# A fused attention and feed-forward kernel: the first twelve chunks' k and q loaded as groups of 512 tokens

## The chip, the cores and the metric

The kernel runs on one core of a Trainium2 chip. Its time is the device time of one execution in microseconds (us); the number compared is the median of several runs. The core has five engines, each of which works through its own list of instructions in order: TensorE (PE, matrix products; PEld is its weight load), VectorE (DVE), ScalarE (ACT), GpSimd (POOL) and SyncE (SP). They wait for each other through semaphores. DMA transfers are issued from SP, ACT or POOL and are carried by 16 DMA engines. Matrix products are written to PSUM, a small memory next to TensorE; everything else lies in SBUF.

## The reference

The reference is sliding-window causal attention over 8 batches, 8 heads, 576 tokens and a head size of 64, followed by a feed-forward layer with a squared relu:

```python
scores = scale * np.matmul(q, k.transpose(0, 1, 3, 2))
rel = pos[:, None] - pos[None, :]
mask = (rel >= 0) & (rel < 64)
scores = np.where(mask, scores, -1e9)
attn = np.exp(scores - np.max(scores, axis=-1, keepdims=True))
attn = attn / (np.sum(attn, axis=-1, keepdims=True) + 1e-09)
attn_out = np.matmul(attn, v)
x = attn_out.transpose(0, 2, 1, 3).reshape(4608, 512)
h = np.maximum(x @ w_in, 0.0)        # w_in: 512 x 2048
out = h * h @ w_out                  # w_out: 2048 x 512
```

All inputs and the output are float32. q, k and v lie in memory as [batch, head, token, 64], so one token of one head is a run of 256 bytes, and consecutive tokens of one head follow each other.

## The kernel before, in words

The 4,608 tokens are worked in 36 *chunks* of 128 tokens; four chunks are a *group* of 512 tokens (9 groups). A chunk goes through these functions, whose short names are used in the order of the work:

- `load` (L77) issues the transfer of one chunk of k, q or v (256 KB: 128 partitions, one token each, with 8 runs of 256 bytes) into a staging tile `st` from a pool of 15. A chunk that crosses a batch boundary takes two transfers of 64 partitions.
- `cast_kq` (L94) and `cast_v` (L101) turn them into float16. `cast_v` has three POOL instructions per chunk: the values, and two copies moved by 64 partitions for the neighbouring window block.
- `transposes` (T, L158) brings k and q of a chunk to head-size-on-partitions with eight TensorE transposes; DVE copies kT and ACT copies qT out of PSUM, 512 elements per partition each. Every fourth chunk fills a boundary tile `kB`, which joins the last 64 keys of the group before with the first 64 of this one.
- `scores` (S, L183) makes 16 small products, two exponentials on ACT and two maskings (a minimum) on DVE.
- `values` (V, L208) multiplies by v with a column of ones for the denominator; DVE takes the reciprocal and multiplies.
- `to_xT` (X, L229) transposes the result back with TensorE, and DVE copies it out. From group 3 on this is a DMA transpose (`to_xT_xbar`), and from group 4 on k and q are transposed by DMA too (`transposes_xbar`).
- The up projection is `up_chunk` (U, L262: one chunk and one quarter of the 2,048 columns, 16 matmuls of 128 columns) for the first eight chunks, and `up` (L253: a whole group and 128 columns, 4 matmuls of 512 columns) later. Both end in `square`: relu on ACT, then a multiply on DVE. `up_chunk` writes to the pool `ps_up` of two PSUM banks, and for odd quarters of the chunks below 6 to `ps_out`'s two banks as well.
- `out_proj` (L281) takes one chunk and one quarter of `w_out`: 4 matmuls of 512 columns. After the fourth quarter ACT copies the sum out and SP issues the store.

Nothing reorders the work: on every engine the instructions stand in the order in which the program calls these functions. The first part is written out by hand. It issues the loads of chunks 0 to 3 in the order k, q, v per chunk (the first q from ACT's queue), then goes through chunks 0 to 5 with `warm` matmuls (products of zeros that keep TensorE busy) in the gaps. The four quarters of w_in and of w_out are loaded from POOL's queue (`load_w_in` L116, `load_w_out` L121; read as float32, written as float16, 1 MB read each), between the POOL casts; the first three quarters of w_in stand behind the casts of v of chunks 0 to 2 and of k of chunk 3. Then `run` (L365) sorts a list of (place, function, arguments) by place, a number between 0 and 1, and calls them: one such list for the out projection of group 0 with the attention of chunks 6 to 11 and the up projection of chunks 6 and 7 (L372 to L380), and one list per later group (L381 to L404), in which `out_proj` of one group alternates with `up` of the next and the attention of the one after.

A staging tile, an `st`, can be loaded again when its cast has read it, and the queue of SP stands still while the instruction at its head waits.

Of the kernel before, what the change touches and what calls it, by code (L numbers as in the profile page):

```python
# [16 lines left out]
def kernel(  # L17
# [37 lines left out]

    NV = 8
    FQ = DFF // 4
    KQ_XBAR = 4
    X_XBAR = 3

# [16 lines left out]
    def load(src, i, eng=None):  # L77

        st = stage.tile([P, H, D], FP32, name="st", tag="st")
        for (p0, p1, b, t0) in pieces(i):  # L80
            (eng or nc.sync).dma_start(  # L81
                out=st[p0:p1], in_=src[b, :, t0:t0 + p1 - p0, :].rearrange("h p d -> p h d"))
        return st

    kqs, kTs, kBs, qTs = {}, {}, {}, {}

    def group_tile(d, pool, key, g, shape, nm):
        if (key, g) not in d:
            d[key, g] = pool.tile(shape, FP16, name=nm, tag=nm)
        return d[key, g]  # L90
# [5 lines left out]
    def cast_kq(key, i, st, copy):  # L96

        copy(out=kq16(key, i // 4)[:, :, i % 4, :].rearrange("p a (b d) -> p a b d", d=D),  # L98
             in_=st[:].rearrange("p (a b) d -> p a b d", b=2))

    def cast_v(i, st):  # L101

        v_ev, v_od, v_next = v_evs[i % NV], v_ods[i % NV], v_ods[(i + 1) % NV]
        nc.gpsimd.tensor_copy(out=v_ev[:, :, 0:D], in_=st[:])  # L104
        nc.gpsimd.tensor_copy(out=v_od[64:P, :, 0:D], in_=v_ev[0:64, :, 0:D])  # L105
        if i + 1 < NCK:
            nc.gpsimd.tensor_copy(out=v_next[0:64, :, 0:D], in_=v_ev[64:P, :, 0:D])  # L107
# [31 lines left out]
        return group_tile(xTs, xtp, "x", g, [P, 2, DMC, 256], "xT")  # L139

    def kT_of(g):
        new = ("k", g) not in kTs
        t = group_tile(kTs, ktp, "k", g, [P, HP, 512], "kT")
        if new:
            kB = group_tile(kBs, ktp, "b", g, [P, HP, P], "kB")
            if g >= KQ_XBAR:
                pass
            elif g > 0:
                nc.vector.tensor_copy(out=kB[:, :, 0:64], in_=kTs["k", g - 1][:, :, 448:512])
            else:  # L150
                nc.vector.memset(kB[:, :, 0:64], 0.0)
        return t

    def qT_of(g):

        return group_tile(qTs, ktp, "q", g, [P, HP, 512], "qT")

    def transposes(i):  # L158
        g, a = i // 4, i % 4 * P
        ps = ps_att.tile([P, 2, 4, P], FP16, name="qkT_ps", tag="ps_a")  # L160
        for s, key in enumerate("kq"):
            for c in range(4):
                nc.tensor.transpose(out=ps[:, s, c, :], in_=kqs[key, g][:, c, i % 4, :],
                                    identity=ident[:])
# [3 lines left out]
        nc.scalar.activation(out=q_dst, in_=q_src, func=AF.Copy, scale=1.0)  # L168
        if i % 4 == 0:
            nc.vector.tensor_copy(out=kBs["b", g][:, :, 64:P], in_=kTs["k", g][:, :, 0:64])  # L170

    def transposes_xbar(g):
        for key, dst in (("k", kT_of(g)), ("q", qT_of(g))):
# [2 lines left out]
                in_=kqs[key, g][:].rearrange("p a c t -> p (a c t)"))  # L176

    def boundary(g):
        kB = kBs["b", g]
        nc.vector.tensor_copy(out=kB[:, :, 0:64], in_=kTs["k", g - 1][:, :, 448:512])  # L180
        nc.vector.tensor_copy(out=kB[:, :, 64:P], in_=kTs["k", g][:, :, 0:64])

    def scores(i):  # L183
# [77 lines left out]

    def up_chunk(i, fq):  # L262
        g, t0, a = i // 4, i % 4 * P, i % 2 * P
        pool, tag = (ps_out, "ps_o") if fq % 2 and i < 6 else (ps_up, "ps_u")
        hps = pool.tile([P, 4, P], FP32, name="hps4", tag=tag)
        for f in range(4):
            for c in range(DMC):
                nc.tensor.matmul(  # L268
                    hps[:, f, :], w_in_q[fq][:, c, f * P:(f + 1) * P],
                    xT_of(g)[:, i % 4 // 2, c, a:a + P], start=(c == 0), stop=(c == DMC - 1))  # L270
# [31 lines left out]
    for i in range(1, 4):  # L302
        sts[i] = [load(x, i) for x in (k, q, v)]
    make_identity(nc, ident[:])
    nc.gpsimd.memset(base[:], BIG)
    nc.gpsimd.affine_select(
# [14 lines left out]
    warm(8)  # L321
    cast_kq("k", 0, sts[0][0], nc.vector.tensor_copy)
    cast_kq("q", 0, sts[0][1], nc.scalar.copy)
    cast_v(0, sts[0][2])

    def cast_chunk(i):
        cast_kq("k", i, sts[i][0], nc.gpsimd.tensor_copy)
        cast_kq("q", i, sts[i][1], nc.scalar.copy)
        cast_v(i, sts[i][2])

    T, S, V, X, U = transposes, scores, values, to_xT, up_chunk
    T(0), warm(3)
    cast_chunk(1)
    S(0), warm(3), T(1), warm(1)
    cast_chunk(2)
    V(0), S(1), warm(2), X(0), T(2), warm(1)
    cast_kq("k", 3, sts[3][0], nc.gpsimd.tensor_copy)
    for quar in range(3):
        load_w_in(quar)
    cast_kq("q", 3, sts[3][1], nc.scalar.copy)  # L340
    cast_v(3, sts[3][2])
    sts[4] = [load(x, 4) for x in (k, q, v)]
    cast_kq("k", 4, sts[4][0], nc.gpsimd.tensor_copy)
    load_w_in(3)
    cast_kq("q", 4, sts[4][1], nc.gpsimd.tensor_copy)
    cast_v(4, sts[4][2])
    sts[5] = [load(x, 5) for x in (k, q, v)]
    cast_kq("k", 5, sts[5][0], nc.gpsimd.tensor_copy)
    load_w_out(0)
    load_w_out(1)  # L350
    cast_kq("q", 5, sts[5][1], nc.gpsimd.tensor_copy)
    cast_v(5, sts[5][2])
    load_w_out(2)
    load_w_out(3)
    V(1), S(2), X(1), warm(1), T(3), V(2), S(3), U(0, 0), X(2), U(1, 0), U(2, 0), V(3)
    load_chunk(6)
    U(0, 1), U(1, 1), X(3), U(2, 1), U(0, 2), U(1, 2), U(2, 2), U(3, 0), U(3, 1), T(4)
    load_chunk(7)
    U(3, 2), U(0, 3), S(4), U(1, 3), U(2, 3), U(3, 3), V(4), T(5), X(4), S(5)
    load_chunk(8)  # L360
    U(4, 0), U(4, 1), U(4, 2), V(5), U(4, 3), X(5), U(5, 0), U(5, 1), U(5, 2), U(5, 3)
    load_chunk(9)
    load_chunk(10)

    def run(steps):  # L365

# [3 lines left out]
            fn(*args)  # L370

    pairs = [(ts, fq) for a in (0, 2) for fq in range(4) for ts in (a, a + 1)]  # L372
    steps = [((n + 0.5) / 16, out_proj, 0, ts, fq) for n, (ts, fq) in enumerate(pairs)]
    for i in range(6, 12):
        t = 0.17 + 0.115 * (i - 6)
        steps += [(t, T, i), (t + 0.06, S, i), (t + 0.15, V, i), (t + 0.21, X, i)]
    steps += [(0.42 + 0.05 * fq, U, 6, fq) for fq in range(4)]
    steps += [(0.65 + 0.05 * fq, U, 7, fq) for fq in range(4)]
    steps += [(0.1 + 0.13 * n, load_chunk, i) for n, i in enumerate(range(11, 16))]
    run(steps)  # L380
    for g in range(2, NTB + 1):  # L381
        G = g + 1
        steps = [((n + 0.5) / 16, out_proj, g - 1, n // 4, n % 4) for n in range(16)]
        if g < NTB:
            steps += [((f + 0.8) / 16, up, g, f) for f in range(FFC)]
        if G < NTB:
            if G >= KQ_XBAR:
                steps += [(0.02, boundary, G), (0.05, S, 4 * G)]
            for j in range(4):
                i, t = 4 * G + j, 0.18 * j  # L390
                if G < KQ_XBAR:
                    steps += [(t, T, i), (t + 0.07, S, i)]
                steps.append((t + 0.17, V, i))
# [12 lines left out]

# [28 lines left out]
```

## Time and profile before

| | |
|---|---|
| median of 3 runs | 335.68 us (334.15 to 335.7) |
| the profiled execution | 335.83 us, of which the span from first to last instruction is 333.8 |
| PE busy | 307.7 us (92%) |
| DVE, ACT, POOL busy | 186.0, 156.3, 116.9 us |
| SP's DMA queue (q1) | 150,128 packets, 45.89 MB |
| POOL's DMA queue (q0: w_in, w_out) | 4,224 packets, 4.19 MB written |
| loads of k, q, v | 256 KB each, 4.7 to 5.2 us from issue to landing (median) |
| w_in, w_out quarters | 10.2 and 10.7 us from issue to landing (median) |

The profile page gives the busy share of each engine in 40 equal slices of the span, in tenths; the row PEclk is the clock that TensorE was granted, and the row DMA the mean busy share of the 16 DMA engines. The chain is the work that ended last, followed back from the end, at each step to what released it; its columns are start, length and what. In a timeline row the columns are start, length, engine, line, operation, out<-in, sizes and count; brackets hold the idle time before it and what ended that. In the table of windows each engine has its busy time and its number of instructions.

### The profile page before, as it was taken

To read this page: it belongs to the slowest core of one execution; us is meant where nothing else is said; L and a number is where in the kernel's file an instruction comes from. 1 tells how busy PE (TensorE), PEld (TensorE's weight loads), DVE (VectorE), ACT (ScalarE), POOL (GpSimd) and SP (SyncE) were. 2 spreads that over 40 slices of the span, in tenths; PEclk is the share of its full clock that TensorE was granted. 3 is DMA by queue.
4 is the path that set the end of the run, shared out by engine and by line. 5 is a ranking of instruction groups with operands and counts; after the bars stand their busy time and mean duration, and the time that the engine had idled before them with its cause. 6 is when DMAs were issued, how large, how long until landed. Compare 5 with 4: busy or idle time off the path is not lost.

```text
span 333.8 us, 7260 instructions
## 1 busy us (share of the span) xinstructions
PE 307.7 (92%) x2883; PEld 166.2 (50%) x2883; DVE 186.0 (56%) x431; ACT 156.3 (47%) x274; POOL 116.9 (35%) x191
## 2 busy tenths in 40 slices
PE   6749968999899999999999999999999999999995
PEld 2438857566644544444454444444444444444442
DVE  4645676478766664674476466647574665444300
ACT  3533553454645454454454455445544564344411
POOL 3761914876607160626063315423460000000000
PEclk9787998999999999999999999999999999999999
DMA  9999999999449769968979796989599121200111
GB/s 170 218 182 209 184 189 219 212 197 222 93 117 168 164 120 234 180 148 185 229 136 222 150 229 125 222 162 230 120 187 213 40 63 22 74 31 33 54 73 63
DMA packets 155425, 50.80 MB, mean 152 GB/s; under 512 B 146688, under 2 KB 150784, under 8 KB 155392
## 3 DMA queue, kind: packets, MB, share of 16 engines
q1 hardware_dynamic: 150128, 45.89, 67.7%
q0 software_dynamic: 4224, 4.19, 7.8%
q8 instruction: 22, 0.36, 0.5%
q10 hardware_dynamic: 1040, 0.26, 0.4%
q14 instruction: 11, 0.09, 0.1%
HBM read 36.70 MB, written 9.44 MB: 138 GB/s over the span
## 4 chain that ended last, share of the span: by engine, by line
PE 58%; DMA 14%; DVE 11%; SPq 7%; ACT 4%; POOL 2%; issue 2%; ACTq 0%; POOLq 0%
PE ops L285 26%; PE hps L256 20%; DMA qT<-q 7%; PE hps L268 7%; DMA st<-in_v_dram 5%; SPq L81 4%; DVE h L250 4%; ACT hrelu L249 3%; PE sc L193 3%; PE av L217 3%; DVE pm L206 2%; DVE x_sb L222 2%; SPq L174 2%; DMA w_in<-in_moe_w_in_dram 2%; POOL v_ev L104 1%
## 5 line engine op out<-in xcount | busy, mean ns | idle before, releaser
L250 DVE SCALAR_TENSOR_TENSOR h<-hps,hrelu 128x512 f16<-128x512 f32 x144 | 99.1, 690 | 109.7 <-ACT hrelu L249 109.3
L285 PE MATMUL ops<-w_out,h 128*128 128x512 f16 x576 | 145.5, 379 | 0.6 <-DVE h L250 0.6
L249 ACT ACTIVATE hrelu<-hps 128x512 f32<-128x512 f32 x144 | 86.0, 598 | 101.0 <-PE hps L256 81.6
L256 PE MATMUL hps<-xT,w_in 128*128 128x512 f16 x448 | 115.1, 379 | 0.0
L285 PEld LDWEIGHTS <-h 128*128 128x128 f16 x576 | 53.8, 98 | 61.4 <-issue 0.8
L256 PEld LDWEIGHTS <-w_in 128*128 128x128 f16 x448 | 42.8, 98 | 50.1
L98 POOL CAST k<-st 128x512 f16<-128x512 f32 x35 | 21.6, 617 | 73.8 <-DMA st<-in_k_dram 61.4
L202 ACT ACTIVATE pm<-sc 128x512 f16<-128x512 f32 x72 | 39.1, 596 | 15.1 <-PE sc L193 14.5
L268 PE MATMUL hps<-xT,w_in 128*128 128x128 f16 x512 | 35.8, 233 | 6.1 <-DMA w_in<-in_moe_w_in_dram 3.3
L104 POOL CAST v_ev<-st 128x512 f16<-128x512 f32 x36 | 23.6, 656 | 42.5 <-DMA st<-in_v_dram 36.9
L268 PEld LDWEIGHTS <-w_in 128*128 128x128 f16 x512 | 33.2, 106 | 8.0 <-issue 3.7
L206 DVE TENSOR_TENSOR pm<-pm,mask_inner 128x512 f16<-128x512 f16 x56 | 29.0, 539 | 8.4 <-ACT pm L202 7.9
L291 ACT ACTIVATE osb<-ops 128x512 f32<-128x512 f32 x36 | 21.5, 599 | 24.8 <-PE ops L285 24.8
L222 DVE TENSOR_TENSOR x_sb<-av,rden 128x256 f16<-128x256 f32 x72 | 30.5, 424 | 2.5
L98 POOL CAST q<-st 128x512 f16<-128x512 f32 x32 | 19.9, 623 | 12.2 <-DMA st<-in_q_dram 11.5
L107 POOL COPY v_od<-v_ev 64x512 f16<-64x512 f16 x35 | 22.7, 650 | 2.0
L105 POOL COPY v_od<-v_ev 64x512 f16<-64x512 f16 x36 | 22.5, 625 | 2.3
L168 ACT ACTIVATE qT<-qkT_ps 128x512 f16<-128x512 f16 x16 | 9.6, 597 | 27.5 <-DVE kT L167 27.5
L217 PEld LDWEIGHTS <-pm 128*64 128x64 f16 x576 | 12.5, 111 | 14.5 <-issue 8.9
L217 PE MATMUL av<-v_od,pm 128*64 128x65 f16 x288 | 16.8, 198 | 1.3 <-DVE pm L206 1.1
L193 PE MATMUL sc<-qT,kT 64*128 64x64 f16 x504 | 14.6, 192 | 3.1 <-ACT qT L168 1.6
L217 PE MATMUL av<-v_ev,pm 128*64 128x65 f16 x288 | 16.8, 198 | 0.0
(46 smaller groups left out, 110.1 us busy)
## 6 DMA issues: line engine op xcount, KB each, us to landing
out_dram<-osb SPq DMA_DIRECT2D x36, 256.0 KB, 2.6
st<-in_k_dram SPq DMA_DIRECT2D x32, 256.0 KB, 4.7
st<-in_v_dram SPq DMA_DIRECT2D x32, 256.0 KB, 5.2
st<-in_q_dram SPq DMA_DIRECT2D x31, 256.0 KB, 4.9
w_in<-in_moe_w_in_dram POOLq DMA_DIRECT2D x4, 512.0 KB, 10.2
w_out<-in_moe_w_out_dram POOLq DMA_DIRECT2D x4, 512.0 KB, 10.7
st<-in_k_dram SPq DMA_DIRECT2D x8, 128.0 KB, 4.2
st<-in_q_dram SPq DMA_DIRECT2D x8, 128.0 KB, 4.2
```

The costliest lines, as they stand in the source:

```text
L98: copy(out=kq16(key, i // 4)[:, :, i % 4, :].rearrange("p a (b d) -> p a b d", d=D), in_=st[:].rearrange("p (a b) d -> p a b d", b=2))
L104: nc.gpsimd.tensor_copy(out=v_ev[:, :, 0:D], in_=st[:])
L193: nc.tensor.matmul(sc[hh][:, hp, blk, :], keys, qTs["q", g][r0:r0 + 64, hp, a + 64 * blk:a + 64 * blk + 64], start=True, stop=True)
L202: nc.scalar.activation(out=pm[:], in_=sc[hh][:], func=AF.Exp, scale=1.0 / float(D) ** 0.5)
L206: nc.vector.tensor_tensor(out=pm[:], in0=pm[:], in1=mask, op=ALU.min)
L217: nc.tensor.matmul(av[64 * blk:64 * blk + 64, h % 4, 0:65], pms[i][h % 2][:, h // 2, blk, :], vv[:, h, 0:65], start=True, stop=True)
L222: nc.vector.tensor_tensor(out=x_sb[:, 2 * half:2 * half + 2, i % 2, :].rearrange("p c (b d) -> p c b d", d=D), in0=av[:, :, 0:D].rearrange ...
L249: nc.scalar.activation(out=hrelu, in_=hps, func=AF.Relu, scale=H_SCALE)
L250: nc.vector.scalar_tensor_tensor(out=out, in0=hps, scalar=0.0, in1=hrelu, op0=ALU.max, op1=ALU.mult)
L256: nc.tensor.matmul(hps[:], w_in_q[f // 4][:, c, f % 4 * P:(f % 4 + 1) * P], xT_of(g)[:, :, c, :], start=(c == 0), stop=(c == DMC - 1))
L268: nc.tensor.matmul(hps[:, f, :], w_in_q[fq][:, c, f * P:(f + 1) * P], xT_of(g)[:, i % 4 // 2, c, a:a + P], start=(c == 0), stop=(c == DMC ...
L285: nc.tensor.matmul(hold[ts % 2][:], h2s["h", g][:, 4 * fq + f, ts * P:(ts + 1) * P], w_out_q[fq][:, f, :], start=(fq == 0 and f == 0), sto ...
```

## The change

- k and q of groups 0, 1 and 2 (chunks 0 to 11) are loaded by a new function, `load_kq`, for a whole group: a partition holds four consecutive tokens of each of the 8 heads, so a run is 1 KB, and a transfer moves 1 MB. Where a group crosses a batch boundary it takes two transfers (16 and 112 partitions for group 1, 32 and 96 for group 2). These tiles come from a new pool of two; the staging pool shrinks from 15 to 12 tiles.
- `cast_run` casts half a group's heads (two instructions of 512 elements), on ACT and DVE for group 0 and on POOL for groups 1 and 2.
- `transposes_run` (TR) replaces `transposes`: it transposes half the heads of one tensor of a group (8 transposes), and one copy of 1,024 elements per partition puts the tokens back in order, reading PSUM at a stride of 128 elements. Of the twelve copies, ten are on ACT and two on DVE.
- `boundary` now makes the boundary tile for every group.
- The hand-written order of the first part is new: k and q of group 0, then v of chunks 0 to 3; the first three quarters of w_in behind the v casts of chunks 0 and 1; the transposes of a whole group ahead of its scores; the up projection of chunks 0 to 3 ahead of the values of chunk 4. The first list of `run` now holds the out projection of group 0 from place 0.2 on, V, X and U of chunks 4 to 7, and the attention of chunks 8 to 11 near its end.
- `up_chunk` uses the additional banks for chunks below 4 instead of 6; `transposes_xbar` moves from place 0.93 to 0.88 in the later lists.

```diff
-    stage = ctx.enter_context(tc.tile_pool(name="stage", bufs=15))
+    stage = ctx.enter_context(tc.tile_pool(name="stage", bufs=12))
+    kqst = ctx.enter_context(tc.tile_pool(name="kqst", bufs=2))
...
+    def load_kq(src, g):
+
+        st = kqst.tile([P, H, 4 * D], FP32, name="kq_st", tag="kq_st")
+        p = 0
+        while p < P:
+            b, t0 = divmod(512 * g + 4 * p, 64 * NB)
+            n = min(P - p, (64 * NB - t0) // 4)
+            nc.sync.dma_start(
+                out=st[p:p + n],
+                in_=src[b, :, t0:t0 + 4 * n, :].rearrange("h (t r) d -> t h (r d)", r=4))
+            p += n
+        return st
...
+    def cast_run(key, g, st, half, copy):
+
+        for a in (2 * half, 2 * half + 1):
+            copy(out=kq16(key, g)[:, a].rearrange("p r (b d) -> p b r d", d=D),
+                 in_=st[:, 2 * a:2 * a + 2, :].rearrange("p b (r d) -> p b r d", d=D))
...
+    def transposes_run(key, g, half, copy):
+
+        ps = ps_att.tile([P, 2, 4, P], FP16, name="run_ps", tag="ps_a")
+        for a in range(2):
+            for r in range(4):
+                nc.tensor.transpose(out=ps[:, a, r, :], in_=kqs[key, g][:, 2 * half + a, r, :],
+                                    identity=ident[:])
+        dst = kT_of(g) if key == "k" else qT_of(g)
+        copy(out=dst[:, 2 * half:2 * half + 2, :].rearrange("p a (t r) -> p a t r", r=4),
+             in_=ps[:].rearrange("p a r t -> p a t r"))
...
-        pool, tag = (ps_out, "ps_o") if fq % 2 and i < 6 else (ps_up, "ps_u")
+        pool, tag = (ps_out, "ps_o") if fq % 2 and i < 4 else (ps_up, "ps_u")
...
-    sts = {0: [load(k, 0), load(q, 0, nc.scalar), load(v, 0)]}
+    kst, qst, vst = {}, {}, {}
+    kst[0], qst[0] = load_kq(k, 0), load_kq(q, 0)
+    for i in range(4):
+        vst[i] = load(v, i)
...
+    warm(14)
+    cast_run("k", 0, kst[0], 0, acopy)
+    cast_run("k", 0, kst[0], 1, vcopy)
+    TR("k", 0, 0, acopy)
+    TR("k", 0, 1, vcopy)
+    warm(3)
+    cast_run("q", 0, qst[0], 0, acopy)
+    cast_run("q", 0, qst[0], 1, vcopy)
+    boundary(0)
+    TR("q", 0, 0, acopy)
+    TR("q", 0, 1, vcopy)
+    for i in range(2):
+        cast_v(i, vst[i])
+    for quar in range(3):
+        load_w_in(quar)
+    for i in range(2, 4):
+        cast_v(i, vst[i])
+    kst[1], qst[1] = load_kq(k, 1), load_kq(q, 1)
+    for i in range(4, 8):
+        vst[i] = load(v, i)
+    for half in range(2):
+        cast_run("k", 1, kst[1], half, pcopy)
+    load_w_in(3)
+    for half in range(2):
+        cast_run("q", 1, qst[1], half, pcopy)
+    warm(2), S(0), warm(2), S(1), warm(3)
+    V(0), S(2), warm(2), X(0), V(1), S(3), X(1), warm(1), V(2), U(0, 0), X(2), V(3), U(1, 0)
+    U(2, 0), X(3), U(0, 1), U(1, 1), U(2, 1), U(3, 0), U(3, 1), U(0, 2), U(1, 2), TR("k", 1, 0, acopy)
+    U(2, 2), TR("k", 1, 1, acopy)
+    boundary(1)
+    U(3, 2), TR("q", 1, 0, acopy)
+    for i in range(4, 8):
+        cast_v(i, vst[i])
+        if i > 4:
+            load_w_out(i - 5)
+    load_w_out(3)
+    U(0, 3), TR("q", 1, 1, acopy), U(1, 3), S(4), U(2, 3), S(5), U(3, 3)
+    kst[2], qst[2] = load_kq(k, 2), load_kq(q, 2)
+    for i in range(8, 12):
+        vst[i] = load(v, i)
...
-    steps = [((n + 0.5) / 16, out_proj, 0, ts, fq) for n, (ts, fq) in enumerate(pairs)]
-    for i in range(6, 12):
-        t = 0.17 + 0.115 * (i - 6)
-        steps += [(t, T, i), (t + 0.06, S, i), (t + 0.15, V, i), (t + 0.21, X, i)]
-    steps += [(0.42 + 0.05 * fq, U, 6, fq) for fq in range(4)]
-    steps += [(0.65 + 0.05 * fq, U, 7, fq) for fq in range(4)]
-    steps += [(0.1 + 0.13 * n, load_chunk, i) for n, i in enumerate(range(11, 16))]
+    steps = [(0.2 + 0.8 * (n + 0.5) / 16, out_proj, 0, ts, fq)
+             for n, (ts, fq) in enumerate(pairs)]
+    for j in range(4):
+        steps += [(0.01 + 0.08 * j, V, 4 + j), (0.05 + 0.08 * j, X, 4 + j)]
+        steps += [(0.07 + 0.15 * j + 0.03 * fq, U, 4 + j, fq) for fq in range(4)]
+        steps += [(0.65 + 0.08 * j, S, 8 + j), (0.71 + 0.08 * j, V, 8 + j),
+                  (0.75 + 0.08 * j, X, 8 + j)]
+        steps += [(0.3 + 0.15 * j, load_chunk, 12 + j)]
+        steps += [(0.55 + 0.02 * j, TR, "kkqq"[j], 2, j % 2, acopy)]
+        steps += [(0.1, cast_vi, 8 + j)]
+    steps += [(0.6, boundary, 2), (0.02, S, 6), (0.1, S, 7)]
...
-                steps.append((0.93, transposes_xbar, g + 2))
+                steps.append((0.88, transposes_xbar, g + 2))
```

More of the change, by code (lines that the diff above doesn't have):

```diff
@@ L57 @@
     FQ = DFF // 4
+    KQ_RUN = 3
     KQ_XBAR = 4
@@ L141, in kT_of @@
     def kT_of(g):
[L142 to L152, printed above, removed]
+        return group_tile(kTs, ktp, "k", g, [P, HP, 512], "kT")
     def qT_of(g):
@@ L169, in transposes @@
         if i % 4 == 0:
-            nc.vector.tensor_copy(out=kBs["b", g][:, :, 64:P], in_=kTs["k", g][:, :, 0:64])
+            boundary(g)
+    def transposes_run(key, g, half, copy):
[7 more added lines that the diff above has]
+             in_=ps[:].rearrange("p a r t -> p a t r"))
     def transposes_xbar(g):
@@ L178, in boundary @@
     def boundary(g):
-        kB = kBs["b", g]
-        nc.vector.tensor_copy(out=kB[:, :, 0:64], in_=kTs["k", g - 1][:, :, 448:512])
+        kB = group_tile(kBs, ktp, "b", g, [P, HP, P], "kB")
+        if g > 0:
+            nc.vector.tensor_copy(out=kB[:, :, 0:64], in_=kTs["k", g - 1][:, :, 448:512])
+        else:
+            nc.vector.memset(kB[:, :, 0:64], 0.0)
         nc.vector.tensor_copy(out=kB[:, :, 64:P], in_=kTs["k", g][:, :, 0:64])
@@ L299 @@
     nc.vector.memset(gate[:], 0.0)
-    sts = {0: [load(k, 0), load(q, 0, nc.scalar), load(v, 0)]}
+    kst, qst, vst = {}, {}, {}
+    kst[0], qst[0] = load_kq(k, 0), load_kq(q, 0)
+    for i in range(4):
+        vst[i] = load(v, i)
     nc.scalar.activation(out=gate[:], in_=gate[:], func=AF.Exp)
-    for i in range(1, 4):
-        sts[i] = [load(x, i) for x in (k, q, v)]
     make_identity(nc, ident[:])
@@ L320 @@
     mask_second = make_mask("mask_second", 1)
[L321 to L335, printed above, removed]
@@ L336 @@
-    V(0), S(1), warm(2), X(0), T(2), warm(1)
-    cast_kq("k", 3, sts[3][0], nc.gpsimd.tensor_copy)
+    T, S, V, X, U, TR = transposes, scores, values, to_xT, up_chunk, transposes_run
+    vcopy, acopy, pcopy = nc.vector.tensor_copy, nc.scalar.copy, nc.gpsimd.tensor_copy
+    warm(14)
[6 more added lines that the diff above has]
+    cast_run("q", 0, qst[0], 1, vcopy)
@@ L338 @@
+    boundary(0)
[3 more added lines that the diff above has]
+        cast_v(i, vst[i])
     for quar in range(3):
         load_w_in(quar)
[L340 to L343, printed above, removed]
-    load_w_in(3)
[L345 to L353, printed above, removed]
-    load_w_out(3)
[L355 to L361, printed above, removed]
@@ L362 @@
-    load_chunk(9)
-    load_chunk(10)
+    for i in range(2, 4):
[5 more added lines that the diff above has]
+        cast_run("k", 1, kst[1], half, pcopy)
+    load_w_in(3)
+    for half in range(2):
+        cast_run("q", 1, qst[1], half, pcopy)
+    warm(2), S(0), warm(2), S(1), warm(3)
+    V(0), S(2), warm(2), X(0), V(1), S(3), X(1), warm(1), V(2), U(0, 0), X(2), V(3), U(1, 0)
@@ new lines @@
+    U(2, 0), X(3), U(0, 1), U(1, 1), U(2, 1), U(3, 0), U(3, 1), U(0, 2), U(1, 2), TR("k", 1, 0, acopy)
[6 more added lines that the diff above has]
+            load_w_out(i - 5)
+    load_w_out(3)
+    U(0, 3), TR("q", 1, 1, acopy), U(1, 3), S(4), U(2, 3), S(5), U(3, 3)
+    kst[2], qst[2] = load_kq(k, 2), load_kq(q, 2)
+    for i in range(8, 12):
+        vst[i] = load(v, i)
+    for half in range(2):
+        cast_run("k", 2, kst[2], half, pcopy)
@@ L365, in run, with cast_vi @@
+    for half in range(2):
+        cast_run("q", 2, qst[2], half, pcopy)
+    def cast_vi(i):
+        cast_v(i, vst[i])
     def run(steps):
```

## The prediction

> **What bounds the kernel now.** I read the page first, for where each engine is full:
>
> ```profile
> span 333.8 us, 7260 instructions
> ...
> PE   6749968999899999999999999999999999999995
> ...
> PEclk9787998999999999999999999999999999999999
> DMA  9999999999449769968979796989599121200111
> ...
> q1 hardware_dynamic: 150128, 45.89, 67.7%
> q0 software_dynamic: 4224, 4.19, 7.8%
> ```
>
> TensorE is full from about slice 12. Ahead of it the DMA engines are full and TensorE has holes, some at a lower clock. So the change can only act in the first 100 us. The chain in order of time says what sets the start:
>
> ```profile
> 8.69 5.13 DMA st<-in_v_dram
> ...
> 16.14 0.56 POOL k L98
> 16.70 6.63 DMA w_in<-in_moe_w_in_dram
> ...
> 23.38 1.89 PE hps L268 x16
> ```
>
> The first up projection (`up_chunk`, U below) waits for w_in; its issue stood on POOL's queue behind casts that wait for the third chunk's loads. After 23.38 no DMA is on this chain until 127. The windows of three early stages (first U at 23.38, end of U(3,3) at 44.94, first `up` at 97.0) and the rest:
>
> ```profile
> 0.00:23.38 23.38, 13.88 (x171) 7.70 (x172) 12.53 (x53) 10.36 (x18) 14.90 (x29) 0.89 1.16 190
> 23.38:44.94 21.56, 19.62 (x308) 18.58 (x310) 13.07 (x26) 10.21 (x18) 9.47 (x15) 0.88 1.14 194
> 44.94:97.02 52.08, 45.23 (x662) 32.49 (x662) 34.65 (x84) 23.55 (x43) 30.07 (x48) 0.97 0.87 176
> 97.02:333.80 236.78, 229.02 (x1749) 107.38 (x1747) 125.76 (x270) 112.22 (x196) 62.42 (x99) 1.00 0.67 140
> ```
>
> The columns after the length are busy PE, PEld, DVE, ACT, POOL, then clock, DMA share, GB/s. I call the stages A, B, C and D. The last view is TensorE in order of time:
>
> ```profile
> 23.38 1.89 PE L268 MATMUL hps<-xT,w_in 128*128 128x128 f16 x16 [3.34 <-DMA w_in<-in_moe_w_in_dram]
> ...
> 46.91 0.29 PE L232 MATMUL xt_ps<-ident,x_sb 128*128 128x128 f16 x2 [1.03 <-DVE x_sb L222]
> ...
> 48.41 0.41 PE L193 MATMUL sc<-qT,kT 64*128 64x64 f16 x16 [0.67 <-ACT qT L168]
> 48.75 4.48 PE L268 MATMUL hps<-xT,w_in 128*128 128x128 f16 x48
> ```
>
> The first row is the wait for w_in. The others are stage C's kind of loss: TensorE waits for attention steps that stand first in its order, and then runs most of 48 matmuls at half clock.
>
> [...] from 22.5 to 31 us, 76 loads and 76 w_in packets start in each half microsecond. [...] 256 B packets take 18 ns, 2 KB packets 85. [...] The trace has half clock at 11.5 to 14.9, 21.7 to 28.6 and 49.0 to 52.5.
>
> **The change, part by part.** (1) *Loads.* 24 loads of 256 KB (1,024 packets of 256 B each) become six of 1 MB (1,024 packets of 1 KB each, four of the six issued in two pieces). Loads land 1.2 us apart: POOL's v casts start at 6.64, 10.26, 13.87, three loads each. A 1 KB packet is not in the trace. A line through 18 and 85 ns gives 47; the lower bound is an eighth of the 8 KB packets' 314 ns, 39; the upper is four small packets, 72. I take 47: 1,024 x 47 / 16 = 3.0 us for 1 MB, where four loads took 4.8. Six times 1.8 is 11 us of DMA time, but stages B and C are not on the DMA chain, so only the start is paid.
>
> (2) *Start, stage A.* k and q now arrive for 512 tokens before any v. The first k was issued at 0.81 and used at 4.73, with q beside it: 1.5 us beyond two loads of 1.2; from the first v (6.64, three loads) it is 2.2. With 1.7: k lands at 0.8 + 1.7 + 3.0 = 5.5, q at 8.5, v0 at 9.7, v1 at 10.9. q is cast (ACT, two at 0.62, pipelined 1.15), transposed (8 matmuls, 0.5) and copied (1.0): S(0) at 11.3 against 7.62, later by 3.7. On POOL the w_in issue moves ahead, behind v0 and v1 only: three casts per chunk, 0.66 each, so 9.7 + 2.0, + 2.0 = 13.7 against 16.70, 3.0 earlier. Before, landing took 6.64 from issue; now k1 and q1 stand beside it, a pair of packets costing 133 ns (96 + 47 less the 10 that overlap before) instead of 105: 512 x 28 / 16 = 0.9 more. So 13.7 + 6.6 + 0.9 = 21.2; I take 21.5. Attention is ready just before: S(0) at 11.3, V(0) 2.9 later (as 7.62 to 10.65 before), V(1) at 17, X(1) at 19.3, V(2) ends at 20. The 8 added warm-up matmuls fill waits there. First U 1.9 us earlier.
>
> (3) *Stage B.* Work before: 16 U at 0.90 (16 x 56 ns) = 14.4; X, X, V, T, S = 0.23 + 0.23 + 0.43 + 0.45 + 0.42 = 1.8; half clock from 23.4 to 28.6 loses 2.6; the remaining 2.8 are waits. After: 14.4; four transposes by group (TR, 0.45 each), two S, V, two X = 3.5; one half-clock window, 1.7, since 21.7 to 25.1 is now full; waits 1.4, since fewer V and DVE copies stand between: 21.0 instead of 21.6. Ends at 42.5, earlier by 2.5. The later w_in quarters land 3.4 us apart beside 256 B packets, 4.3 beside 1 KB ones (512 pairs each): 25.8, 29.2, 32.6; they are needed at 26, 31 and 37: hidden. q1 (landed near 23, needed at 37) and w_out (issued near 35 behind v5's cast, landed 7.7 later as the first one before, needed at 55) are hidden too. If that cover were gone, each us late would be one on TensorE.
>
> (4) *Stage C.* Moved out: TR replaces seven T (3.15 to 1.8 us) and one S (0.4): minus 1.75. DVE loses seven kT copies (0.42 each, 2.9 us); ACT's seven qT copies of 0.6 become four of 1,024. That copy reads PSUM at a stride. [...] Bounds: 0.6 and, if the stride costs, 2.0. Two of DVE's are in stage A, 0.7 to 1.2, beside ACT's of the same length. Waits: the new order has V and X of chunk 4, and again of chunk 6, with next to nothing between: reciprocal and multiply twice (1.1), then the xT copy 0.4, and semaphores: 2.0 each, 4.0. At the end S(i) to V(i) has one `out_proj` step (0.87) under a latency of 1.6 (exp 0.6, 0.5; mask 0.5): 0.7 x 4 = 2.8. That is 6.8, and before's stage C has 52.08 - 45.23 = 6.85. U(4) and U(5) lose two of four PSUM banks (`i < 4`): two banks turn in 0.9 + 0.6 + 0.69 + 0.1 = 2.3 us, 1.15 per U instead of 0.90; for half of these eight, +1.0, of which some lies in the waits: +0.6. One more half-clock window, out of those waits: +1.7. Sum: -1.75 + 0 + 0.6 + 1.7 = +0.6.
>
> (5) *Stage D* keeps its order on every engine (the transposes at 0.88 instead of 0.93 pass nothing on SP). 12 staging tiles instead of 15 are one round of its loop. I take nothing: its casts free tiles as loads land; without that cover it would show as loads waiting for POOL, about 1 us per round.
>
> Sum: -1.9 - 0.6 + 0.6 = -1.9 us on the profiled 335.83 (span 333.8 and 2.0 around it): 333.9. The median of runs is 0.15 lower: 333.8.
>
> **Rivals.** *R1, more gain:* the 1 KB packet is at 40 ns, and no window of stage C falls to half clock: another 1.7 + 0.8, 331.2. For it: 8 KB packets at 314 ns; against: the wait rows above. *R2, the start is hidden anyway:* w_in takes the whole of the lead in sharing the engines with 1 MB loads; first U at 23.4, and the other stages cancel: 335.7. For it: the first w_out took 7.7 us to land; against: w_in ran nearly alone for 2 us after its start. *R3, slower, ACT becomes the bound:* the strided copy of 1,024 at 2.0 us. Eight of them in stages B and C, each ahead of the exp or relu that TensorE waits for: 8 x 1.0 x 0.75 = 6 more, 339.8; it decides from about 1.3 us per copy. For it: no 16-bit read of that stride in the trace. *R4, the change doesn't do what it says:* 1 KB packets cost 72 ns. Then q lands at 11.7, v1 at 14.1, w_in's issue at 16.9, its landing 8.2 later (25.1): first U 1.7 late, 337.4. For it: four times the bytes; against: 2 KB packets at 85.
>
> **How the numbers follow.** Forecast 0.45 (own range 332.4 to 335.2, split 0.27 faster, 0.18 same), R1 0.13 faster, R2 0.17 (0.15 same, 0.02 slower), R3 0.13 slower, R4 0.12 (0.02 same, 0.10 slower). Within 0.5% (334.0 to 337.4) is about what a measurement of this kernel can't tell from no change: the three runs span 0.46%. Faster 0.40, same 0.35, slower 0.25. The range 330.5 to 338.5 leaves out most of R3 and the far end of R1.
>
> **What would show it.** First w_in issue near 13.7 and first U near 21.5 (24 or later: R4 or R2); loads of 1,024 B at 47 ns (72: R4); `run_ps` copies on ACT at 1.03 us (over 1.3: R3); U(3,3) done near 42.5; half clock at 21.7 for one window instead of two; waits of 1 to 2 us before the X of chunks 4 and 6; first `up` at 95. Stage D longer than 237 us would make me wrong where I costed nothing.

## The result, and the profile after

The changed kernel takes 338.75 us (median of 4 runs, 337.84 to 339.33) where the kernel before, beside it, takes 334.97 (4 runs): a ratio of 1.0111, 95% interval 1.0071 to 1.0152. The forecast was 333.8, with a range up to 338.5. The profiled execution took 339.33 us, its span 337.3: 3.5 us more than the span before.

The page after, in the rows shown of the page before:

```profile
span 337.3 us, 7237 instructions
...
PE   7728987799899999999999999999999999999994
...
PEclk9976997799999999999999999999999999999999
DMA  7999999942929569958989796989589021100111
...
q1 hardware_dynamic: 132480, 46.15, 65.2%
q0 software_dynamic: 4224, 4.19, 7.3%
```

SP's queue has 17,648 packets fewer, and the 1,040 of the first q on ACT's queue are gone too; the DMA engines are less busy, as meant. TensorE's hole in slice 3 is deeper (2 tenths, before 4), and the clock is low in slices 3 and 4 and again in 7 and 8. The stages by the same events as before (first U, end of U(3,3), first `up`); columns are length, busy PE, PEld, DVE, ACT, POOL, clock, DMA share, GB/s:

```profile
0.00:26.87 26.87, 14.66 (x180) 7.23 (x180) 13.92 (x54) 10.02 (x16) 14.32 (x29) 0.91 1.07 224
26.87:48.43 21.56, 20.81 (x345) 19.80 (x345) 13.16 (x25) 13.80 (x23) 13.77 (x22) 0.88 1.16 213
48.43:99.47 51.04, 44.16 (x622) 31.44 (x621) 30.80 (x77) 22.59 (x39) 23.25 (x39) 0.93 0.74 141
99.47:337.30 237.83, 229.04 (x1749) 107.36 (x1747) 125.61 (x270) 112.23 (x196) 62.03 (x99) 1.00 0.65 139
```

Against the table before: A +3.49, B 0.00, C -1.04, D +1.05, together +3.50. The loss is the start. D's +1.05 is not in its loop: from the first `up` to the last `osb` copy on ACT it takes 232.84 us before (97.02 to 329.86) and 232.93 after (99.47 to 332.40). The rest lies from that copy on, in the last store and the end of the program: 3.91 us before, 4.86 after, and 3.5 to 4.9 in the edits of the changed kernel below, so that it differs from run to run. Why is open.

The chain that leads to the first U, in order of time (start, length, what):

```profile
1.94 8.61 DMA st<-in_v_dram
10.60 0.62 POOL v_ev L125
...
13.95 0.64 POOL v_od L128
14.59 12.23 DMA w_in<-in_moe_w_in_dram
26.87 1.89 PE hps L293 x16
```

w_in is issued at 14.59 instead of 16.70, as the new order wants, but takes 12.23 us to land where it took 6.63. TensorE in order of time shows that wait and those of stage C (brackets: idle time and what ended it):

```profile
26.87 1.89 PE L293 MATMUL hps<-xT,w_in 128*128 128x128 f16 x16 [7.15 <-DMA w_in<-in_moe_w_in_dram]
...
51.38 0.28 PE L257 MATMUL xt_ps<-ident,x_sb 128*128 128x128 f16 x2 [2.16 <-DVE x_sb L247]
...
61.06 0.28 PE L257 MATMUL xt_ps<-ident,x_sb 128*128 128x128 f16 x2 [1.59 <-DVE x_sb L247]
```

Where do the 12.23 us go? The packet records split them: the first w_in packet starts at 21.43, 6.84 us after the issue, and the quarter then lands in 5.4. Before, it was 1.85 and 4.8. So what grew is the wait ahead of w_in's first packet. The view of the DMA queues (packets, MB, share of 16 engines), for the time from w_in's issue to its first packet, before (16.70 to 18.55):

```profile
DMA packets 971, 0.24 MB, mean 130 GB/s; under 512 B 970, under 2 KB 971, under 8 KB 971
...
q1 hardware_dynamic: 970, 0.24, 86.9%
q0 software_dynamic: 1, 0.00, 0.3%
```

and after (14.59 to 21.43):

```profile
DMA packets 1348, 1.36 MB, mean 199 GB/s; under 512 B 33, under 2 KB 1347, under 8 KB 1347
...
q1 hardware_dynamic: 1346, 1.34, 112.0%
...
q0 software_dynamic: 1, 0.00, 0.1%
```

In both, SP's queue (q1) sends about a thousand packets before POOL's queue (q0) sends its first. Before they are 256 B packets; after they are k and q of group 1, more than five times the bytes, and they move at 199 GB/s although all engines are full. Group 0's packets, the same 1 KB, ran at 355 GB/s (3.0 to 8.5 us). That gives two suspects: what stands in SP's queue ahead of w_in, and the pieces of 16 and 112 partitions in which group 1 is issued.

Not all of the wait is a full queue, though. Before, from 17.5 to 18.25 us, the engines were less than half busy, and w_in still did not start:

```profile
DMA packets 211, 0.05 MB, mean 69 GB/s; under 512 B 211, under 2 KB 211, under 8 KB 211
...
q1 hardware_dynamic: 211, 0.05, 43.7%
```

In both kernels the instruction that issues w_in takes 0.87 us of the wait on POOL itself; how the rest of the 1.85 us before divides is open.

### The profile page after: what moved, and what is told of

Read it like the earlier page. It is cut to its first block, busy times and chain, and to the rows that moved or that the text cites. A ratio compares the mean times of both kernels' runs of the same rounds, so it can differ in the third digit from the quotient of the medians.

```text
span 337.3 us, 7237 instructions
## 1 busy us (share of the span) xinstructions
PE 308.7 (92%) x2891; PEld 165.8 (49%) x2891; DVE 183.5 (54%) x424; ACT 158.6 (47%) x272; POOL 113.4 (34%) x188
## 4 chain that ended last, share of the span: by engine, by line
PE 59%; DMA 19%; DVE 7%; ACT 6%; SPq 5%; POOL 2%; issue 2%; POOLq 0%; ACTq 0%
PE ops L310 26%; PE hps L281 19%; DMA qT<-q 7%; PE hps L293 7%; DMA st<-in_v_dram 7%; DMA w_in<-in_moe_w_in_dram 4%; PE av L242 3%; PE sc L218 3%; DVE h L275 3%; ACT hrelu L274 2%; SPq L196 2%; DVE pm L231 2%; ACT pm L227 1%; DVE x_sb L247 1%; ACT qT L191 1%
## 5 line engine op out<-in xcount | busy, mean ns | idle before, releaser
L227 ACT ACTIVATE pm<-sc 128x512 f16<-128x512 f32 x72 | 39.0, 597 | 22.4 <-PE sc L218 21.8
L293 PE MATMUL hps<-xT,w_in 128*128 128x128 f16 x512 | 36.6, 233 | 8.4 <-DMA w_in<-in_moe_w_in_dram 7.1
L113 POOL CAST k<-st 128x512 f16<-128x512 f32 x24 | 14.9, 620 | 83.4 <-DMA st<-in_k_dram 71.9
L125 POOL CAST v_ev<-st 128x512 f16<-128x512 f32 x36 | 22.6, 629 | 35.3 <-DMA st<-in_v_dram 28.5
L231 DVE TENSOR_TENSOR pm<-pm,mask_inner 128x512 f16<-128x512 f16 x56 | 26.6, 499 | 4.5 <-ACT pm L227 4.1
L126 POOL COPY v_od<-v_ev 64x512 f16<-64x512 f16 x36 | 22.5, 624 | 2.3
L113 POOL CAST q<-st 128x512 f16<-128x512 f32 x24 | 14.8, 618 | 9.7 <-DMA st<-in_q_dram 9.7
L218 PEld LDWEIGHTS <-kT 64*128 64x128 f16 x504 | 10.7, 95 | 4.1 <-issue 2.7
```

The lines of the kernel that those rows point to most:

```text
L218: nc.tensor.matmul(sc[hh][:, hp, blk, :], keys, qTs["q", g][r0:r0 + 64, hp, a + 64 * blk:a + 64 * blk + 64], start=True, stop=True)
L227: nc.scalar.activation(out=pm[:], in_=sc[hh][:], func=AF.Exp, scale=1.0 / float(D) ** 0.5)
L231: nc.vector.tensor_tensor(out=pm[:], in0=pm[:], in1=mask, op=ALU.min)
L293: nc.tensor.matmul(hps[:, f, :], w_in_q[fq][:, c, f * P:(f + 1) * P], xT_of(g)[:, i % 4 // 2, c, a:a + P], start=(c == 0), stop=(c == DMC ...
```

## The experiments

The ratio is to the kernel before, run beside it on the same chip; the median of that kernel was 334.97 for the change and 335.66, 335.91, 335.45 or (one run, for the cut by heads) 336.52 us for the edits, so medians of different rows compare only through the ratio. "First packet" is w_in's; "first U" and "first `up`" are from the profiled execution. Letters for theories belong to the expectation in which they stand.

| run | median us | ratio, 95% interval | w_in issued | first packet | first U | first `up` |
|---|---|---|---|---|---|---|
| before | 334.97 | 1 | 16.70 | 18.55 | 23.38 | 97.0 |
| after | 338.75 | 1.0111 (1.0071 to 1.0152) | 14.59 | 21.43 | 26.87 | 99.5 |
| two v loads ahead | 338.04 | 1.0081 (1.0045 to 1.0118) | 14.53 | 20.6 | 26.98 | 99.1 |
| four v loads ahead | 337.99 | 1.0071 (1.0039 to 1.0104) | 14.54 | 17.57 | 23.51 | 98.5 |
| group 0 cut 16+112, 32+96 | 339.55 (one run) | | 17.21 | 23.4 | 29.16 | 100.8 |
| group 0 cut 64+64 | 340.18 (one run) | | 18.70 | 25.16 | 30.52 | 101.3 |
| group 0 cut by heads | 338.75 (one run) | | 14.88 | 21.24 | 26.95 | 99.5 |
| group 1 whole | 336.35 | 1.0022 (1.0004 to 1.0040) | 14.90 | 19.54 | 24.75 | 96.6 |
| group 1 in 256 B | 335.48 | 1.0005 (0.9984 to 1.0026) | 14.57 | 17.98 | 23.13 | 96.1 |
| groups 1, 2 in 256 B | 335.96 | 1.0018 (1.0004 to 1.0033) | 14.93 | 18.08 | 23.58 | 96.3 |
| all groups in 256 B | 337.87 | 1.0075 (1.0043 to 1.0107) | 17.81 | 21.18 | 26.27 | 100.5 |
| four v ahead, w_in early | 341.89 | 1.0199 (1.0148 to 1.0251) | 12.73 | 15.73 | 20.71 | 102.5 |
| group 1 in 256 B, w_in early | 336.92 | 1.0065 (1.0039 to 1.0091) | 12.84 | 15.46 | 21.01 | 95.8 |
| before, w_in early | 332.48 | 0.9923 (0.9881 to 0.9966) | 12.38 | 14.98 | 21.48 | 94.0 |

### What stands ahead of w_in in SP's queue

**Two v loads ahead.**

```diff
+    for i in range(4, 6):
+        vst[i] = load(v, i)
     kst[1], qst[1] = load_kq(k, 1), load_kq(q, 1)
-    for i in range(4, 8):
+    for i in range(6, 8):
         vst[i] = load(v, i)
```

> The changed kernel with v of chunks 4 and 5 issued ahead of k and q of group 1 on SP's queue; nothing else. In the changed kernel w_in's first packet moves 6.4 us after its issue (14.6 to 21.0) and the first quarter lands at 26.8. Theory Q (w_in waits for the about 1,000 packets that SP has already handed to the DMA engines, whatever their size; here those are packets of 256 B at 18 ns instead of 1 KB at 72): first w_in packet 1.9 to 2.5 us after its issue, first quarter landed at 21 to 22.5, first up projection by 22.5, time 4 us below the changed kernel, 334.5. Theory G (w_in is slow to start for a reason on POOL's side, not for what stands ahead of it): first packet still 6 us after its issue, first up projection at 26 to 27, time as the changed kernel, 338.5.

Measured: no gain at the start, first U at 26.98, which are the numbers of theory G. But the edit was too small to decide: much of the two loads had gone by when w_in was issued, and 2,095 packets of SP's queue with 1.32 MB still went ahead of it, nearly as many bytes as in the change itself (1.34). It shows that the wait is not set by a number of packets, as theory Q had it: 2,095 passed in 6.07 us, 1,346 in 6.84.

**Group 1 in 256 B runs**, the order unchanged (`load_kq` issues four transfers for each piece, one per token of a run, for g == 1; the order of the words in the staging tile, and the cast that reads it, change with it):

```diff
+            if g == 1:
+                for r in range(4):
+                    nc.sync.dma_start(
+                        out=st[p:p + n, r],
+                        in_=src[b, :, t0:t0 + 4 * n, :].rearrange(
+                            "h (t r) d -> t r h d", r=4)[:, r])
```

> The changed kernel with k and q of group 1 alone loaded in runs of 256 B (four times the packets, same order, same casts), group 0 and 2 as changed. Theory Q: about 1,000 packets of 256 B stand ahead of w_in, so its first packet moves 2 us after its issue, the first quarter lands at 21 to 22.5 and the first up projection starts by 22.5; q of group 1 then lands 8 us or more later than in the changed kernel (28.6) and w_in's fourth quarter, issued behind k's casts, lands near 40, so that stage B grows by several us and the time is between 334 and 340. Theory G: first up projection at 26 to 27 all the same, time above the changed kernel.

The queues from w_in's issue to its first packet (14.57 to 18.0), and TensorE's wait:

```profile
q1 hardware_dynamic: 2298, 0.58, 137.7%
...
q0 software_dynamic: 1, 0.00, 0.2%
```

```profile
23.13 1.89 PE L304 MATMUL hps<-xT,w_in 128*128 128x128 f16 x16 [3.44 <-DMA w_in<-in_moe_w_in_dram]
```

2,298 packets go first, more than in the change, but with 0.58 MB: 3.41 us instead of 6.84. The first U comes 3.7 us sooner and the whole loss is gone. So the 1 KB runs of group 1 alone turn the result.

**Four v loads ahead.**

```diff
-    kst[1], qst[1] = load_kq(k, 1), load_kq(q, 1)
     for i in range(4, 8):
         vst[i] = load(v, i)
+    kst[1], qst[1] = load_kq(k, 1), load_kq(q, 1)
```

> Edit to the changed kernel: the loads of v of chunks 4 to 7 go to SP's queue ahead of k and q of group 1. Order on every other engine, packet sizes and pieces stay. Theory Q (w_in waits for what SP has queued ahead of it, and the 1 KB packets make that queue three times longer in time): w_in is issued at about 14.5 as before the edit, the queue ahead of it is now mostly 256 B packets, its first packet comes at 17 (2.2 to 3.4 after the issue, not 6.8), the first U at 22 to 23, first up at 95.5, about 335. Theory G (1 KB packets of group 1 take the bandwidth wherever they stand): the first U stays past 26, about 338.

The queue ahead of w_in is now 256 B packets, with packet sizes and pieces as in the change (14.54 to 17.57):

```profile
DMA packets 2464, 0.64 MB, mean 210 GB/s; under 512 B 2463, under 2 KB 2463, under 8 KB 2463
```

First packet after 3.03 us instead of 6.84, first U at 23.51 (0.5 later than the queue theory said), with the 1 KB loads still in the program. That w_in's wait grows with what SP has queued ahead of it is shown. The time is not 335, because the delay moved on. The chain in order of time:

```profile
16.52 14.24 DMA kq_st<-in_k_dram
...
30.91 2.24 POOL k L119 x4
33.15 8.08 DMA w_in<-in_moe_w_in_dram
41.23 0.05 issue
41.27 1.08 PE hps L293 x16
```

k of group 1 lands at 30.8, its POOL casts stand ahead of the fourth quarter's issue, and TensorE waits 2.05 us for that quarter.

### Why the pieces are slow

**Group 0 cut in pieces** like those of the other groups:

```diff
+            if g == 0 and p == 0:
+                n = 16 if src is k else 32
```

> The changed kernel with k of group 0 loaded in two pieces of 16 and 112 partitions and q of group 0 in two of 32 and 96, as groups 1 and 2 are, where nothing else is on the DMA engines. In the changed kernel k and q of group 0, whole, land at 6.27 and 9.34, with packets of 46 ns, and those of group 1, in pieces, have packets of 72 ns. Theory P (pieces that are not 128 partitions make the packets slow): packets of 70 ns or more, k lands at 8 or later, q at 12 or later. Theory C (company of other transfers makes them slow, not the pieces): packets of 46 ns, k lands at 6.3 to 6.8, q at 9.4 to 10.2.

k landed at 7.38 and q at 12.36 (whole: 6.27 and 9.34); the median packet went from 46 to 69 ns. Same data, same packets, only cut.

**Cut evenly, and cut by heads.** Is it the odd sizes, any cut, or having 512 packets in a transfer?

```diff
+            if g == 0 and p == 0:
+                n = 64
```

> Edit to the changed kernel: k and q of group 0 are each loaded in two pieces of 64 partitions, where the change loads them whole; the same 1 KB packets, the same data. If any cut makes 1 KB packets slow, group 0 lands as with cuts of 16+112 and 32+96 (q at 12, packets at 67 ns, w_in issued at 17, first U at 29). If it is the odd cut, packets stay at 46 to 50 ns, q lands at 9.4 to 10 and the first U at 27.

and by heads (the source takes the same heads):

```diff
+            for h in ((0, 4), (4, 8)) if g == 0 else ((0, 8),):
                 nc.sync.dma_start(
-                    out=st[p:p + n],
+                    out=st[p:p + n, h[0]:h[1]],
```

> Edit to the changed kernel: k and q of group 0 are each loaded in two DMAs of four heads, each over all 128 partitions, instead of one of eight heads. Same 1 KB packets, 512 per DMA as with the cut into 64+64 partitions. If fewer partitions per DMA make the packets slow, they stay at 46 to 50 ns here, q lands at 9.4 to 10, first U at 27. If a DMA of 512 packets is slow as such, they take 86 ns as with 64+64, q lands at 13, first U at 30.

The queues while group 0 loads, cut in 64+64 partitions (4 to 11 us):

```profile
DMA packets 1505, 1.49 MB, mean 213 GB/s; under 512 B 48, under 2 KB 1505, under 8 KB 1505
```

and cut by heads, each transfer over all 128 partitions (4 to 8.5 us):

```profile
DMA packets 1696, 1.56 MB, mean 346 GB/s; under 512 B 217, under 2 KB 1696, under 8 KB 1696
```

With 64 partitions a transfer the median packet is 86 ns and q lands at 13.44; by heads it is 46 ns and 9.56, and the first U comes at 26.95 (uncut 26.87). So it is neither a cut as such nor the number of packets in a transfer: over 64 partitions the same data goes slower, at 213 GB/s instead of 346. What makes it so the records do not show.

The change's piece of 112 partitions ran slower than a whole transfer, too (15.75 to 18.5 us; group 0 whole: 355 GB/s):

```profile
DMA packets 681, 0.69 MB, mean 250 GB/s; under 512 B 9, under 2 KB 681, under 8 KB 681
```

Its start was slower still, 98 GB/s from 14.7 to 15.2 us; by 14.7 276 packets of 1 KB had started, more than twice as many as the piece of 16 ahead of it holds. Whether that piece holds up the one behind it, and why 64, 96 and 112 partitions are slow, is open.

**Group 1 whole.** Group 1 reads the tokens of group 0, so that it needs no pieces; the 1 KB runs and the order stay, and chunks 4 to 7 compute on other tokens.

```diff
-            b, t0 = divmod(512 * g + 4 * p, 64 * NB)
+            b, t0 = divmod(512 * (g if g != 1 else 0) + 4 * p, 64 * NB)
```

> Edit to the changed kernel: group 1 of k and q is read from the tokens of group 0, so that each is one DMA over 128 partitions and no pieces of 16 and 112; the outputs of chunks 4 to 7 are then computed on other tokens, the work is the same. 1 KB packets stay. Theory P (pieces slow the packets to 72 to 85 ns): packets of group 1 fall to about 47 ns alone, and w_in's first packet comes 4 us after its issue instead of 6.8, the first U at 24, about 336. Rival (it is the 1 KB packet beside the traffic of w_in and v, not the piece): 72 ns and more stay, first U at 26.9, 338.7.

From w_in's issue to its first packet (14.90 to 19.54), and TensorE:

```profile
DMA packets 1646, 1.61 MB, mean 348 GB/s; under 512 B 107, under 2 KB 1645, under 8 KB 1645
```

```profile
24.75 1.89 PE L293 MATMUL hps<-xT,w_in 128*128 128x128 f16 x16 [4.72 <-DMA w_in<-in_moe_w_in_dram]
```

Packets at 51 ns, 348 GB/s instead of 199, and although more bytes go first, the wait is 4.64 us instead of 6.84; the first U is 2.1 us sooner and the time within 0.5% of before. Both suspects count: with group 1 whole the wait is still 2.8 us longer than before; the pieces add 2.2.

### What the rest of the change is worth

**All groups in 256 B, and groups 1 and 2.** The condition of the edit above becomes `g < 3` and `g in (1, 2)`.

> Edit to the changed kernel: all three groups of k and q load in 256 B runs (four DMAs per piece, one per token of a run), order laid out as in the change. Undoes the 1 KB runs and keeps the rest. If the 1 KB runs of group 0 earn at the start what their shorter transfer says (k0 and q0 3.0 us each instead of 4.8), then against the kernel with group 1 alone at 256 B the v casts, w_in's issue and the first U come 3 to 3.6 us later (issue 18, first U 26.5) and the time is 338.5. Rival: the queue ahead of w_in sets the start whatever group 0 takes, first U within 1 us of 23.1, 335.5.

> Edit to the changed kernel: groups 1 and 2 of k and q in 256 B runs, group 0 alone in 1 KB runs. Group 2 and w_out stand behind nothing that is late, so the size of group 2's packets is hidden: first U at 23.1, first up at 96, 335.5 as with group 1 alone at 256 B. Rival: group 2 costs stage C 1.3 us (that stage was 52.2 long with all three groups at 256 B, 50.9 with group 1 alone): first up at 97.4, 336.8.

Without any 1 KB run w_in is issued at 17.81 and the first U is at 26.27 (ratio 1.0075): the new order alone is slower, since the whole first group of k and q comes ahead of the first v. Its chain:

```profile
8.61 5.14 DMA st<-in_v_dram
...
17.17 0.64 POOL v_od L139
17.81 8.42 DMA w_in<-in_moe_w_in_dram
26.22 0.05 issue
26.27 1.89 PE hps L304 x16
```

With group 0 in 1 KB runs the issue is 2.9 us sooner and the first U 2.7 (1.0018); group 2 adds nothing that these intervals tell (1.0005); group 1 then costs 1.06% (1.0111). In round numbers: order +2.5 us, group 0's runs -1.9, group 1's +3.6.

**w_in issued earlier.** The three quarters go behind the v cast of chunk 0 in two of the kernels above:

```diff
-    for i in range(2):
-        cast_v(i, vst[i])
+    cast_v(0, vst[0])
     for quar in range(3):
         load_w_in(quar)
-    for i in range(2, 4):
+    for i in range(1, 4):
         cast_v(i, vst[i])
```

and in the kernel before behind the casts of chunk 1, instead of those of chunk 2 and of k of chunk 3:

```diff
     cast_chunk(1)
+    for quar in range(3):
+        load_w_in(quar)
     S(0), warm(3), T(1), warm(1)
     cast_chunk(2)
     V(0), S(1), warm(2), X(0), T(2), warm(1)
     cast_kq("k", 3, sts[3][0], nc.gpsimd.tensor_copy)
-    for quar in range(3):
-        load_w_in(quar)
```

> Edit to the changed kernel: as the run with four v loads ahead, and the three w_in quarters are issued behind the v cast of chunk 0 instead of chunk 1. If the landing of w_in sets the first U, issue at 12.5, first packet at 15, first quarter landed at 18.5 to 19; then attention (V of chunk 2) is last and the first U comes at 21; first up at 94, 333. If the queue ahead does not shorten with an earlier issue, first U at 22 to 23 and 335.

> Edit to the kernel with group 1 alone in 256 B runs: the three w_in quarters are issued behind the v cast of chunk 0 instead of chunk 1. Issue at 12.6, first packet at 15.5 to 16, first quarter landed near 20.5, first U at 21 to 21.5 (attention is ready then), first up at 94 to 94.5, 333.5 to 334, faster than before. Rival: k and q of group 1 come later by what w_in comes earlier and TensorE waits for their transposes as in the run with four v loads ahead: first up stays at 96 or later, 335.5 or more.

> The kernel before with the first three w_in quarters issued behind the v cast of chunk 1 instead of behind the k cast of chunk 3, 3.6 us earlier on POOL; loads and order else as before. If a lead of w_in at the start is worth its length (the prediction's stage A): first quarter landed at 19.5 to 20.5, first up projection 2 to 3 us earlier than 23.4, time 332.5. If the third and fourth chunks' loads, now beside w_in, hold the attention that stands ahead of the first up projection: first up projection within 1 us of 23.4 and the time within 1 us of before.

In the new order the first U comes at 20.71 and 21.01, as expected, but the times of 333 to 334 do not follow: both kernels are slower than without the step (1.0199 against 1.0071, 1.0065 against 1.0005). With four v loads ahead, TensorE in order of time:

```profile
35.95 0.40 PE L188 MATMUL run_ps<-ident,k 128*128 128x128 f16 x4 [2.96 <-POOL k L119]
40.14 0.40 PE L188 MATMUL run_ps<-ident,q 128*128 128x128 f16 x4 [1.01 <-POOL q L119]
44.64 1.73 PE L293 MATMUL hps<-xT,w_in 128*128 128x128 f16 x16 [3.54 <-DMA w_in<-in_moe_w_in_dram]
```

k and q of group 1 are needed whole before one transpose of the group can be made, and they lose at least what w_in gains: k of group 1 lands 4.4 us later for a first quarter that lands 2.8 us earlier, and with group 1 in 256 B 2.5 later for 2.1. In the latter kernel the waits for q and for w_in are 1.29 and 1.72 us, and the first `up` (95.8) is where it was (96.1). Its profiled execution took 335.02 us, the lowest of eight; why the median is 1.9 above that is open.

The kernel before has no such group. There the same step moves everything:

```profile
21.48:41.60 20.12, 17.23 (x313) 16.18 (x310) 14.59 (x29) 11.24 (x20) 12.09 (x19) 1.00 1.24 197
41.60:93.98 52.38, 45.14 (x661) 32.48 (x662) 34.12 (x84) 23.54 (x43) 30.73 (x49) 0.97 0.91 184
```

The first U is 1.9 us sooner, stage B is 1.4 shorter, with full clock throughout (0.88 before), and 332.48 us (ratio 0.9923) beats both kernels.

## Why the prediction was wrong

The sum was A -1.9, B -0.6, C +0.6, D 0. It came out as +3.5, 0.0, -1.0, +1.05.

**Part (2), the landing of w_in, is the step that failed.** It took "landing took 6.64 from issue" and added 0.9 for pairs of packets, one of each queue. That prices the time after w_in's first packet, and there it held roughly: 5.4 us where 4.8 + 0.9 = 5.7 was priced (its 76 packets of each queue in half a microsecond hold from about 23 us, not from 22.5). It took over as a constant, without looking at it, the 1.85 us before that packet, and these became 6.84. The runs showed in its place a wait that grows with what SP has queued: 3.0 us with v loads of 256 B ahead, 4.64 with whole 1 KB loads, 6.84 with 1 KB loads in pieces. The trace before had the wait, 970 packets of one queue against one of the other; that it would grow could not be read from it alone, since the engines were half idle at its end. The miss at the first U is 5.4 us (26.87 for 21.5): 0.9 from the issue (14.59 for 13.7), 4.7 from landing (12.23 for 7.5), less the 0.3 by which the forecast rounded up.

**Part (1), the price of a 1 KB packet,** was right for group 0: 46 ns for 47; k landed at 6.27 and q at 9.34 (forecast 5.5 and 8.5: most of the late issue is the first load, 0.8 later than thought). Its lower bound of 39 leaned on a reading that is too low: the 8 KB packets of the trace before take 307 to 655 ns, 484 by median, not 314. It was wrong for the pieces, which it counted and gave no price. 69 to 86 ns is about R4's 72; but R4 put it on group 0, where it would have delayed the issue, and got 337.4 with the first U at 25.1.

**The start of attention** was right within a microsecond: S(0) at 12.05 for 11.3. TensorE then stood idle for 7.15 us ahead of the first U, so the delay of attention lay wholly inside the wait for w_in.

**Part (3), stage B:** 21.56 for 21.0. The forecast had one half-clock window from 21.7; the trace has half clock from 21.8 to 32.0, as long inside the stage (5.1 us) as before, so that term did not fall. TensorE's hole ahead of it is 7.15 us instead of 3.34; that half clock follows from such holes was the author's assumption. The waits fell by 1.2 us (idle time of TensorE 1.94 before, 0.75 after; priced 2.8 and 1.4). That the stage came out within 0.6 us is in part two errors that offset each other.

**Part (4), stage C:** -1.0 for +0.6. The waits before X came as priced (2.16 and 1.59 for 2.0 each), idle time stayed (51.04 - 44.16 = 6.9; before 6.85), and the strided copies on ACT took 1.01 us for 1.03 (the author's estimate), which ends R3. The added half-clock window came too (52.5 to 55.9 and 62.7 to 66.1 us; before 49.0 to 52.5 alone), but its price of 1.7 seems wrong: with group 1 in 256 B that stage has clock 0.97 instead of 0.93, and is 50.86 us long instead of 51.04, with TensorE busy for 42.72 us instead of 44.16. There the slower matmuls stand where TensorE would have waited; that rests on this one pair of kernels. Without the 1.7 the forecast is -1.15; as the bank term of 0.6 in it was not tried by itself, how near that comes may be luck.

**Part (5)** was right on the loop, which has the same length within 0.1 us. Its sign of being wrong, a stage D longer than 237 us, was met all the same (237.83), by the end of the program, which it did not price apart and which differs from run to run.

**The rivals.** R1 and R3 are out: 1 KB packets at 46 ns and not 40, and no copy of 2 us. R2 saw that w_in could lose its lead to the 1 MB loads; by sharing, though, not by standing behind them, and so with no more than the lead lost. The forecast's own sign "24 or later: R4 or R2" was met with a mechanism that neither had.

## What to carry to other kernels

Before moving the issue of a transfer on one queue, count what other queues have already handed to the DMA engines at that moment, in bytes and at the rate at which those bytes move: the new transfer's first packet may start only after many of them (here after some 970 to 2,460, 1.85 to 6.84 us from its issue). In these runs longer runs made a load shorter only where a transfer covered all 128 partitions: from the landing of k to that of q of group 0 it was 3.1 us whole, 5.0 us cut by partitions, and four loads of 256 B runs take 4.8. Cut by heads rather than by partitions where there is a choice (346 GB/s here, against 213 over 64 partitions). And ask of an earlier transfer what it delays: in the order by groups the gain at the first U came back as waits for group 1, in the order by chunks it stayed.

## What the runs showed of the hardware that was not expected

- A transfer issued on POOL's queue sent its first packet only after some 970 to 2,460 packets of SP's queue (1.85 us before, 2.6 to 3.4 us where most of them are of 256 B, 4.6 to 6.8 with 1 KB). A part of this is not the queue: before, SP's packets took 43.7% of the engines' time from 17.5 to 18.25 us, and w_in's first came at 18.55. Afterwards the two queues start about as many packets each, in the change at once (56 to 60 of each in every half microsecond from 21.5 to 24.5), before only from about 23 us (73 to 91 of each from 23.5 to 31). What sets the wait is open.
- SP is well ahead of the engines: at w_in's issue between 1,860 and 2,390 of its packets were issued and not yet started in the changed kernel, between 750 and 1,280 before (a transfer of 528 packets was just being issued). In the change only 1,346 of them passed ahead of w_in, so it does not wait for all that SP has issued.
- 1 KB packets ran at 46 ns over 128 partitions, by median 86 ns over 64 at a time, and 79 ns in the stretch with pieces of 16 and 112.
